# Seven block products for one more group of a fused attention and MLP kernel, with its transposes given to DMA

## The chip, the cores and the metric

The kernel runs on one core of a Trainium2 chip. The metric is the device time of one execution in microseconds. Times of runs are medians; the profile is of one execution, and its span goes from the first to the last instruction.

## The reference

Two layers follow each other. The first is attention with decay, over blocks of 64 positions, for 4 batches, 8 heads, 768 positions and 64 channels. The second normalises the rows of 512 channels and runs a two-layer MLP of width 2048, with a residual:

```
for each block b:
    intra = (q_b k_b^T * Dmask) v_b              # Dmask[i,j] = lam^(i-j) for i >= j, else 0
    inter = (q_b * lam^(pos+1)) @ kv_state
    out_b = intra + inter
    kv_state = lam^64 * kv_state + (k_b * lam^(63-pos))^T v_b
x  = out, heads side by side                     # (4, 768, 512)
xn = (x - mean(x)) / sqrt(var(x) + 1e-6) * g_ln
y  = x + relu(xn @ W1) @ W2                      # W1 512 x 2048, W2 2048 x 512
```

## The kernel before

**Tiling.** The 3072 rows are cut into 12 windows of 256 positions, numbered u = 0 to 11. Window u belongs to batch u mod 4. Each window is a group of two tiles of 128 rows. For each window, attention makes `x` of both tiles, `xc` (centred, times g_ln, bf16) and `xT` (its transpose). Then m1 makes hT = relu(W1^T xT), and m2 multiplies it with W2 and adds x. Windows below 6 (`LB`) use a 128-position form of attention (`kv`, `scores`, `av`, `inter`). Later ones use a 64-position form (`kv64`, `scores64`, `av64`).

**Order.** The order on every engine is written out by hand at the end of the kernel. `plan` is a list of m1 and m2 pieces, called units, of all groups from the second on. `units(n)` issues the next n of them, and the attention steps of later windows stand between such calls. A group has eight m1 units and then eight m2 units. A unit of m1 is 8 matmuls of 256 columns (L530) and one ScalarE relu into hT (L533). The queues of all engines are in order. SP issues nearly all DMAs: loads of k, q and v (`load_in`, L76 and L80), transposes of k and q (`transpose_dma`, L257), transposes of xc (`to_xT`, L486) and stores (L698).

**Attention steps.** The steps `s1` to `s4` treat one window: `s1` has kv and the first scores, `s2` the second scores, `s3` the product with v and the first half of inter, `s4` the second half and the norms. `X1` and `X2` are the same for a later window, with the rest of the window before it. `new_state` and `states64` make the running state: VectorE reads the kv product (`Stmp` L317, or `Smid` L388 and `Stmp` L391), and GpSimd multiplies it with the decay into `Sn` (L313). `reader` copies a few columns of `po` into `seen` (L443), which fences the two halves of inter. `norm` copies po to x on ScalarE (L458) and makes xc on VectorE (L460). `in_k_one`, `in_q_one` and `in_v` cast and scale the loaded inputs into `kq` and `vb` (L231, L236, L242).

**Two forms of m2.** Groups below `WG` use the plain form: for each of the two tiles, 16 matmuls of 512 columns (L666) in four units, and one VectorE eviction of 512 columns (L690). Groups from `WG` on cut h and W2 into 2 x 2 blocks and form seven block products in place of eight:

```python
        products = (("P1", "a", True), ("P2", "b", True), ("P7", "c", True), ("P5", "d", True),
                    ("P6", "a", False), ("P4", "c", False), ("P3", "d", False))
```

A product is 8 matmuls of 256 columns (L565). A unit `m2w(n)` issues 7 of the 56, so a unit's border mostly lies inside a product. The letters are PSUM tiles `pwa` to `pwd`. Each comes from the pool "mm" of four buffers (`mm_tile`), which m1, plain m2, kv and kv64 also use. Three things come in addition. `w_sums(c, n)` forms sums of blocks of W2 once per quarter c (L787 to L791, VectorE, into `wt`). `sums(lo, hi)` (`h_sums`) forms sums of blocks of h for half of the row blocks (L548 to L550, VectorE, into `hs`). `evict` scales each product by rstd and adds it to x (L578 on VectorE; P1 and P7 by ScalarE at L589 and L597, then GpSimd at L590 and L598).

**x^T.** `to_xT` makes it on TensorE for windows below 2 and for those in `X_PE` (four transposes, L493, and a ScalarE copy, L494, for each tile), and else by one DMA transpose for each tile.

Of the kernel before, what the change touches and what calls it, by code (L numbers as in the profile page):

```python
# [17 lines left out]
def kernel(  # L18
# [11 lines left out]
    nc = tc.nc  # L30
# [11 lines left out]
    NWC = 4  # L42
    eps = 1e-6
    XS = 64.0
    WG = 4
    assert D == 64 and S % W == 0 and DM == 512

    ctx.enter_context(tc.manual_schedule())
# [7 lines left out]

    half = [slice(0, 64), slice(64, 128)]
    XB = 3
    X_PE = (2, 3, 4)
    LB = 6  # L60

    def mm_tile(shape, dtype, name):
        return ps.tile(shape, dtype, tag="mm", bufs=4, name=name)
# [8 lines left out]
    def fill(got, name, u, hs, eng=None):  # L72
        eng = eng or nc.sync
        src = dict(k=k, q=q, v=v)[name]
        if u < LB:
            eng.dma_start(got[:, hs], source(src, u, hs))  # L76
            return
        cc, b = divmod(u, B)
        for j in range(2):
            eng.dma_start(got[:, hs, j * D:(j + 1) * D],  # L80
                          src[b, hs, cc * W + j * C:cc * W + (j + 1) * C, :].rearrange("h p d -> p h d"))
# [11 lines left out]
    def load_in(u, name, eng):  # L93
        got = qkv_in[u][name]
        fill(got, name, u, slice(0, H), eng)
        qkv_in[u][name] = got.rearrange("p h (j d) -> p h j d", j=2)
# [54 lines left out]
    def make_keep64():  # L151
        for dst, base in ((keep64, 0), (keep64_b, D)):
            nc.gpsimd.memset(dst, 1.0)
            nc.gpsimd.affine_select(
                out=dst, in_=dst, compare_op=ALU.is_ge, fill=0.0,
                base=base, pattern=[[1, D]], channel_multiplier=-1,
            )
        nc.vector.tensor_copy(keep64[half[1]], keep64_b[half[1]])
# [39 lines left out]
    def open_window(u):  # L198
        kq = wk.tile([128, 2, NP, 2, 2, D], BF16, tag="kq", bufs=3, name="kq")
        vb = wk.tile([128, H, 2, D], BF16, tag="vb", bufs=4, name="vb")  # L200
        st[u] = dict(kq=kq, vb=vb)
        if u < XB:
            st[u]["kqT"] = wk.tile([128, 2, NP, 2, 128], BF16, tag="kqT", bufs=3, name="kqT")

    def part(a, dst, hs):

        return dst[:, a, hs.start // 2:hs.stop // 2].rearrange("p a j e d -> p a e j d")
# [21 lines left out]
    def in_k_one(u, eng, j):  # L229
        src = qkv_in[u]["k"].rearrange("p (a e) j d -> p a e j d", e=2)  # L230
        (eng.copy if eng is nc.scalar else eng.tensor_copy)(part(0, st[u]["kq"], ALL)[:, :, :, j], src[:, :, :, j])  # L231

    def in_q_one(u, eng, j):
        src = qkv_in[u]["q"].rearrange("p (a e) j d -> p a e j d", e=2)
        lq = (lam_q[:, :, j] if u < LB else lam_p[:, 0, :]).rearrange("p (a e) -> p a e", e=2)
        eng.tensor_tensor(part(1, st[u]["kq"], ALL)[:, :, :, j], src[:, :, :, j],  # L236
                          lq[:, :, :, None].to_broadcast([128, NP, 2, D]), op=ALU.mult)
# [200 lines left out]
    def reader(u):  # L438
        s = st[u]
        for ab in range(2):  # L440
            if s["S"][ab][1] is not None:
                seen = wk.tile([128, H], F32, tag="seen", name="seen")
                (nc.scalar.copy if u > WG else nc.vector.tensor_copy)(seen, s["po"][ab][:, :, 0])  # L443

    def norm(u, ab, early=False):
        s = st[u]
# [30 lines left out]
    def to_xT(u, ab):  # L477
        s = st[u]
        t = 2 * u + ab
        g = group_of[t]  # L480
        i = t - groups[g][0]
        if i == 0:
            xT_of[g] = gp.tile([128, KA, GT * 128], BF16, tag="xT", bufs=3, name="xT")
        dst = xT_of[g][:, :, i * 128:(i + 1) * 128]
        if u >= 2 and u not in X_PE:
            nc.sync.dma_start_transpose(dst, s["xc"][:, ab])  # L486
        else:
            if u < 2:
                xt = mm_tile([128, KA, 128], BF16, "xt")
            else:  # L490
                xt = ps.tile([128, KA, 128], BF16, tag=f"po{ab}", name="xt")
            for kk in range(KA):
                nc.tensor.transpose(xt[:, kk, :], s["xc"][:, ab, kk * 128:(kk + 1) * 128], ident)  # L493
            nc.scalar.copy(dst, xt)  # L494
# [18 lines left out]
    m2s = {}  # L513
# [267 lines left out]
    def w_sums(c, n):  # L781
        v = w2[c].rearrange("p (k e) d -> p k e d", e=2)
        w = DM // 2
        b11, b12, b21, b22 = v[:, :, 0, 0:w], v[:, :, 0, w:], v[:, :, 1, 0:w], v[:, :, 1, w:]
        t1, t2, t3, t4 = (wt[c][:, :, i] for i in range(4))
        if n == 0:
            nc.vector.tensor_tensor(t1, b12, b11, op=ALU.subtract)  # L787
            nc.vector.tensor_tensor(t3, b12, b22, op=ALU.add)
        else:
            nc.vector.tensor_tensor(t2, b11, t3, op=ALU.subtract)  # L790
            nc.vector.tensor_tensor(t4, t2, b21, op=ALU.add)  # L791
# [73 lines left out]
    def s2(u):  # L865
        scores(u, 1)
        mask(u, 1)
# [11 lines left out]
    def s4(u):  # L879
        inter(u, 1)  # L880
        if st[u]["S"][0][1] is not None:
            norm(u, 0)
        norm(u, 1)
# [31 lines left out]
    def X2(u):  # L915
        scores64(u)
        inter(u - 1, 1)
        mask64(u, 0)
        norm(u - 1, 0)
        norm(u - 1, 1)  # L920
        mask64(u, 1)
# [20 lines left out]
    in_k(1, nc.gpsimd)  # L942
    norm(0, 0, early=True)
    reader(0)
    behind(qkv_in[1]["k"][:, 0, 0, 0:1])
    load_w1(1)
# [71 lines left out]
    for g in range(2, len(groups)):  # L1018
        m1, m2 = mlp(g)
        plan += [(m1, n) for n in range(m1.count)]  # L1020
        if g >= WG:
            plan += [(m2.w, n) for n in range(8)]
# [5 lines left out]
    def units(n):  # L1028
        for _ in range(n):
            f, *a = next(steps)  # L1030
            f(*a)
# [15 lines left out]
    s3(2)  # L1047
    units(2)
    s4(2)
    open_window(3)  # L1050
    in_k_one(3, nc.vector, 0)
    in_k_one(3, nc.vector, 1)
    in_q_one(3, nc.gpsimd, 0)
    in_q_one(3, nc.gpsimd, 1)
    in_v(3, nc.gpsimd)
# [10 lines left out]
    units(1)  # L1066
    load_in(5, "v", nc.sync)
    units(1)
    open_window(4)
    in_k_one(4, nc.gpsimd, 0)  # L1070
    in_k_one(4, nc.gpsimd, 1)
# [1 line left out]
    in_q_one(4, nc.gpsimd, 1)  # L1073
    in_v(4, nc.gpsimd)
    units(5)
    w_sums(0, 0)
    w_sums(0, 1)
    units(2)
    w_sums(1, 0)
    units(1)  # L1080
    s1(3)
    store(0)
    transpose_dma(4, 0)
    transpose_dma(4, 1)
    units(2)
    s2(3)
    units(1)
    open_window(5)
    in_k_one(5, nc.gpsimd, 0)
# [8 lines left out]
    open_in(6, False)  # L1098
    load_in(6, "k", nc.sync)
    units(1)  # L1100
    load_in(6, "q", nc.sync)
    units(1)
    w_sums(1, 1)
    load_in(6, "v", nc.sync)
    units(1)
    w_sums(2, 0)
    transpose_dma(5, 0)
    units(1)
    make_keep64()
    to_xT(3, 0)  # L1110
    transpose_dma(5, 1)
    open_in(7, False)
    load_in(7, "k", nc.sync)
    units(1)
    w_sums(2, 1)
    s1(4)
    to_xT(3, 1)
    open_window(6)
# [7 lines left out]
    units(2)  # L1126
    s3(4)
    units(1)
    in_q_one(6, nc.vector, 1)
    in_v(6, nc.gpsimd)  # L1130
    s4(4)
    in_q_one(6, nc.vector, 0)
    units(3)
    load_in(7, "q", nc.sync)
    units(1)
    w_sums(3, 0)
    w_sums(3, 1)
    units(1)
    open_in(8, False)
    to_xT(4, 0)  # L1140
    units(1)
    to_xT(4, 1)
    s1(5)
    units(1)
    transpose_dma(6, 1)
# [14 lines left out]
    units(1)  # L1160
    in_k_one(7, nc.scalar, 0)
    units(1)
    X2(6)
    open_window(8)
    units(3)
    m2s[4].sums(0, 4)
    units(1)
    store(1)
# [188 lines left out]
```

## Time and profile before

| what | us |
|---|---|
| median of 4 runs (lowest to highest) | 210.67 (210.46 to 212.09) |
| the profiled execution | 210.66 |
| its span | 208.9 |
| TensorE busy in the span | 198.7 |
| VectorE busy | 138.4 |
| ScalarE busy | 119.0 |
| GpSimd busy | 85.8 |
| mean granted TensorE clock | 0.998 of full speed |

In the profile, PE is TensorE, PEld its weight loads, DVE VectorE, ACT ScalarE, POOL GpSimd and SPq the DMA queue of SP. A row of the timeline has its start and its length in us, the engine, the line, what is written and read with shapes, how many instructions it merges, and in brackets how long the engine was idle before and what ended that. A row of the chain has start, length, what. The chain is followed back from the last instruction, at each step to what released it.

### The profile page before, as it was taken

The page shows a single profiled execution, that of the slowest core. Times are in us where ns is not written, and L with a number is a line of the kernel's source. Part 1 is how long each engine was busy: PE and PEld are TensorE (multiplying, and loading weights), DVE is VectorE, ACT ScalarE, POOL GpSimd, SP SyncE. Part 2 cuts the span into 40 slices and gives each one's busy share as a digit, 9 for nine tenths or more (in the row PEclk, how much of TensorE's full clock was granted, in tenths as well). Part 3 has the DMA queues.
Part 4 walks back from the last instruction along what each step waited for, and adds up shares of the span by engine and source line. Part 5 has one row for each costly group of instructions (what it writes and reads, how often), then busy time and mean ns, then how long its engine had stood idle before and what let it go on. Part 6 is the DMA issues. An engine that isn't in the chain of part 4 may idle for free.

```text
span 208.9 us, 7231 instructions
## 1 busy us (share of the span) xinstructions
PE 198.7 (95%) x3099; PEld 156.6 (75%) x3099; DVE 138.4 (66%) x277; ACT 119.0 (57%) x275; POOL 85.8 (41%) x118
## 2 busy tenths in 40 slices
PE   2889999999999999999999999999999999999992
PEld 0469789545685587478888888888888888888881
DVE  2587580537585776758897776777877947865263
ACT  3834869326254667347566675585596565652620
POOL 4679138219747330626355441782282202011020
PEclk9999999999999999999999999999999999999999
DMA  4999999999999999996899999797958020178403
GB/s 111 297 270 215 201 284 164 192 304 276 186 322 164 219 151 194 192 294 66 175 226 149 196 201 153 195 216 111 236 113 178 3 50 3 25 145 278 111 18 83
DMA packets 91041, 36.38 MB, mean 174 GB/s; under 512 B 65153, under 2 KB 88193, under 8 KB 91010
## 3 DMA queue, kind: packets, MB, share of 16 engines
q1 hardware_dynamic: 86400, 31.53, 74.3%
q0 software_dynamic: 4224, 4.19, 12.7%
q8 instruction: 24, 0.39, 0.8%
q10 hardware_dynamic: 386, 0.20, 0.4%
q14 instruction: 7, 0.06, 0.1%
HBM read 27.27 MB, written 6.29 MB: 161 GB/s over the span
## 4 chain that ended last, share of the span: by engine, by line
PE 78%; DVE 7%; issue 6%; DMA 3%; ACT 2%; POOL 1%; SPq 1%; POOLq 0%; DVEq 0%
PE pm L530 31%; PE pm L666 14%; PE pwa L565 5%; PE pwd L565 5%; PE pwc L565 5%; PE pwb L565 3%; PE pm1t L640 2%; PE po L419 2%; DMA lam_b<-in_lam_dram 2%; PE tp L250 2%; PE po L432 2%; DMA out_dram<-x 1%; PE xt L493 1%; PE sc L273 1%; DVE x L578 1%
## 5 line engine op out<-in xcount | busy, mean ns | idle before, releaser
L530 PE MATMUL pm<-xT,w 128*128 128x256 bf16 x736 | 84.9, 273 | 0.1
L530 PEld LDWEIGHTS <-w 128*128 128x128 bf16 x736 | 70.3, 98 | 9.9 <-issue 0.3
L533 ACT ACTIVATE hT<-pm 128x512 f16<-128x512 f32 x92 | 53.9, 599 | 29.2 <-PE pm L530 29.0
L666 PE MATMUL pm<-w,hT 128*128 128x512 f16 x128 | 30.2, 380 | 0.0
L565 PEld LDWEIGHTS <-hs 128*128 128x128 f16 x256 | 24.9, 98 | 2.9
L313 POOL TENSOR_TENSOR Sn<-Stmp,lam_s 128x256 bf16<-128x256 f32 x16 | 9.8, 616 | 38.6 <-DVE Stmp L317 19.8
L590 POOL TENSOR_TENSOR x<-ev_u,x 128x256 f32<-128x256 f32 x8 | 6.4, 796 | 46.2 <-ACT ev_u L589 46.2
L548 DVE TENSOR_TENSOR hs<-hT 128x1024 f16<-128x1024 f16 x16 | 14.2, 888 | 16.3 <-ACT hT L533 16.3
L565 PEld LDWEIGHTS <-hT 128*128 128x128 f16 x192 | 18.1, 98 | 3.6 <-ACT hT L533 1.6
L666 PEld LDWEIGHTS <-hT 128*128 128x128 f16 x128 | 11.7, 98 | 12.1
L283 DVE TENSOR_TENSOR mA<-sc,keep 128x512 bf16<-128x512 f32 x20 | 13.1, 684 | 6.9 <-PE sc L273 6.9
L458 ACT ACTIVATE x<-po 128x512 f32<-128x512 f32 x18 | 10.6, 590 | 9.7 <-PE po L419 5.3
L460 DVE SCALAR_TENSOR_TENSOR xc<-po,nmean,g_row 128x512 bf16<-128x512 f32 x18 | 12.9, 745 | 3.7 <-ACT nmean L459 3.7
L503 ACT ACTIVATE sq<-x,nmean 128x512 bf16<-128x512 f32 x18 | 12.9, 719 | 0.3
L578 DVE SCALAR_TENSOR_TENSOR x<-pwd,rstd,x 128x256 f32<-128x256 f32 x16 | 7.7, 483 | 8.0 <-POOL x L598 8.0
L242 POOL TENSOR_TENSOR vb<-vin,lam_p 128x1024 bf16<-128x1024 f32 x6 | 11.4, 1898 | 3.2 <-ACT hT L533 3.0
L236 POOL TENSOR_TENSOR kq<-qin,lam_q 128x512 bf16<-128x512 f32 x10 | 10.3, 1046 | 5.7 <-DMA qin<-in_q_dram 5.7
L242 POOL TENSOR_TENSOR vb<-vin,lam_v 128x1024 bf16<-128x1024 f32 (+1 forms) x7 | 11.7, 1675 | 1.4 <-DMA vin<-in_v_dram 1.4
L494 ACT COPY xT<-xt 128x512 bf16<-128x512 bf16 x10 | 5.8, 583 | 9.0 <-PE xt L493 9.0
L550 DVE TENSOR_TENSOR hs<-hs,hT 128x512 f16<-128x512 f16 x16 | 10.1, 628 | 0.5
L578 DVE SCALAR_TENSOR_TENSOR x<-pwa,rstd,x 128x512 f32<-128x512 f32 (+1 forms) x16 | 9.1, 612 | 0.8
L236 POOL TENSOR_TENSOR kq<-qin,lam_p 128x512 bf16<-128x512 f32 x9 | 9.3, 1044 | 1.0 <-DMA qin<-in_q_dram 1.0
(128 smaller groups left out, 300.9 us busy)
## 6 DMA issues: line engine op xcount, KB each, us to landing
out_dram<-x SPq DMA_DIRECT2D x22, 256.0 KB, 3.9
w<-in_moe_w_ch_dram POOLq DMA_DIRECT2D x8, 512.0 KB, 9.2
kin<-in_k_dram SPq DMA_DIRECT2D x14, 256.0 KB, 5.2
qin<-in_q_dram SPq DMA_DIRECT2D x14, 256.0 KB, 5.0
vin<-in_v_dram SPq DMA_DIRECT2D x14, 256.0 KB, 5.2
kin<-in_k_dram SPq DMA_DIRECT2D x5, 512.0 KB, 6.5
qin<-in_q_dram SPq DMA_DIRECT2D x5, 512.0 KB, 8.5
vin<-in_v_dram SPq DMA_DIRECT2D x5, 512.0 KB, 7.8
```

The source lines that it names most:

```text
L236: eng.tensor_tensor(part(1, st[u]["kq"], ALL)[:, :, :, j], src[:, :, :, j], lq[:, :, :, None].to_broadcast([128, NP, 2, D]), op=ALU.mult)
L242: eng.tensor_tensor(st[u]["vb"][:, hs], qkv_in[u]["v"][:, hs], lv.to_broadcast([128, n, 2, D]), op=ALU.mult)
L283: nc.vector.tensor_tensor(s[f"mA{hf}"][:, e], s[f"sc{hf}"][e], kp[:, None, :, :].to_broadcast([128, 2, 2, 128]), op=ALU.mult)
L458: nc.scalar.activation(x, po, ACT.Copy, accum_out=sm)
L460: nc.vector.scalar_tensor_tensor(xc, in0=po, scalar=nm, in1=g_row, op0=ALU.add, op1=ALU.mult)
L503: nc.scalar.activation(sq, s["x"][:, ab], ACT.Square, bias=s["nmean"][:, ab:ab + 1], accum_out=ss[:, ab:ab + 1])
L530: nc.tensor.matmul(pm[:, b, :], lhsT=w1[n // W2K][:, kk, (n % W2K) * 128:(n % W2K + 1) * 128], rhs=xT_of[g][:, kk, 0:N], start=(b == 0 and ...
L533: nc.scalar.activation(hT[:, u * NB:(u + 1) * NB, 0:N], pm, ACT.Relu)
L548: nc.vector.tensor_tensor(s13, b[:, :, 1:2, :].to_broadcast([128, n, 2, 128]), b[:, :, 0:4:3, :], op=ALU.subtract)
L565: nc.tensor.matmul(pr[bank], lhsT=lhs(r), rhs=rhs, start=(first and r == 0), stop=(r == KB // 2 - 1), skip_group_check=True)
L578: nc.vector.scalar_tensor_tensor(out, in0=in0, scalar=r[ab], in1=in1, op0=ALU.mult, op1=ALU.add)
L666: nc.tensor.matmul(acc[i], lhsT=hT[:, kk, i * 128:(i + 1) * 128], rhs=w2[kk // W2K][:, kk % W2K, :], start=(kk == 0), stop=(kk == KB - 1))
```

## The change

From group 3 on (it was 4) m2 has the form of seven products, so windows 3 to 11 use it. The steps of W2's sums stand earlier in the written order and are all issued before the attention of window 4. x^T of window 4 is made by two DMA transposes. With these come other moves. The k casts of window 3 go from VectorE to ScalarE, the q products of window 6 from VectorE to GpSimd, and the fence reads of windows 3 and 4 from VectorE to ScalarE. The DMA transposes of window 4 stand ahead of the load of q of window 7 on SP. `X2(6)` and `open_window(8)` come two units later.

```diff
-    WG = 4
+    WG = 3
...
-    X_PE = (2, 3, 4)
+    X_PE = (2, 3)
...
-                (nc.scalar.copy if u > WG else nc.vector.tensor_copy)(seen, s["po"][ab][:, :, 0])
+                (nc.scalar.copy if u > 2 else nc.vector.tensor_copy)(seen, s["po"][ab][:, :, 0])
...
     s4(2)
+    w_sums(0, 0)
     open_window(3)
-    in_k_one(3, nc.vector, 0)
-    in_k_one(3, nc.vector, 1)
+    in_k_one(3, nc.scalar, 0)
+    in_k_one(3, nc.scalar, 1)
...
     load_in(5, "v", nc.sync)
     units(1)
+    w_sums(0, 1)
     open_window(4)
...
     units(5)
-    w_sums(0, 0)
-    w_sums(0, 1)
-    units(2)
     w_sums(1, 0)
-    units(1)
+    w_sums(1, 1)
+    units(3)
     s1(3)
...
     s2(3)
+    w_sums(2, 0)
     units(1)
...
     load_in(6, "k", nc.sync)
     units(1)
+    w_sums(2, 1)
     load_in(6, "q", nc.sync)
     units(1)
-    w_sums(1, 1)
     load_in(6, "v", nc.sync)
     units(1)
-    w_sums(2, 0)
+    w_sums(3, 0)
     transpose_dma(5, 0)
     units(1)
+    w_sums(3, 1)
     make_keep64()
...
     load_in(7, "k", nc.sync)
     units(1)
-    w_sums(2, 1)
     s1(4)
...
-    in_q_one(6, nc.vector, 1)
+    in_q_one(6, nc.gpsimd, 1)
     in_v(6, nc.gpsimd)
     s4(4)
-    in_q_one(6, nc.vector, 0)
-    units(3)
+    in_q_one(6, nc.gpsimd, 0)
+    units(1)
+    m2s[3].sums(0, 4)
+    units(1)
+    to_xT(4, 0)
+    to_xT(4, 1)
+    units(1)
     load_in(7, "q", nc.sync)
     units(1)
-    w_sums(3, 0)
-    w_sums(3, 1)
+    m2s[3].sums(4, 8)
     units(1)
     open_in(8, False)
-    to_xT(4, 0)
-    units(1)
-    to_xT(4, 1)
+    units(1)
     s1(5)
...
     in_k_one(7, nc.scalar, 0)
     units(1)
+    open_window(8)
+    units(2)
     X2(6)
-    open_window(8)
-    units(3)
+    units(1)
     m2s[4].sums(0, 4)
```

## The prediction

> **What bounds the kernel now.** I read the page's busy line first, then the chain that ended last, then the chain in order of time for the stage that the change rewrites, and at last the timelines of VectorE, GpSimd and the SP queue in that stage.
>
> ```profile
> PE 198.7 (95%) x3099; PEld 156.6 (75%) x3099; DVE 138.4 (66%) x277; ACT 119.0 (57%) x275; POOL 85.8 (41%) x118
> PE 78%; DVE 7%; issue 6%; DMA 3%; ACT 2%; POOL 1%; SPq 1%; POOLq 0%; DVEq 0%
> ```
>
> TensorE is busy 95% of the span and carries 78% of the chain; the rest of the chain lies in the first 15 us and the last 30. A busy TensorE need not be a bound one, so I look whether the chain leaves it in the stage of the change. Columns: start, length, what.
>
> ```profile
> 81.00 0.86 PE pm L666 x4
> 82.09 0.86 PE pm L666 x4
> 83.17 0.38 PE pk L307 x32
> 83.78 2.70 PE pm L666 x12
> 86.82 2.70 PE pm L666 x12
> 89.52 0.64 PE po L419 x64
> 90.59 1.85 PE pm L530 x16
> ...
> 98.52 0.97 PE pwa L565 x8
> 99.49 0.87 PE pwb L565 x8
> ```
>
> It does not: from 81.0 (m1 of the fourth pair, u=3, is done) to 90.59 (m1 of u=4 starts) each piece begins where the last one ends. The 0.23 and 0.22 us holes at 81.86 and 82.95 are the four transposes of x^T each. So here a removed matmul is worth its time, as long as nobody makes TensorE wait. The last two rows show the form that the change brings to this stage: a block product of eight matmuls takes 0.87 us, the first after another kind 0.97.
>
> **The change part by part.** *TensorE, removed and added.* Out go 32 matmuls of 512 columns, 0.86 + 0.86 + 2.70 + 2.70 = 7.12 us, and eight transposes, 0.45 us: 7.57. In come 56 matmuls of 256 columns: 0.97 + 6 x 0.87 = 6.19. Two of the products are cut by attention work of u=5; 2.70 for twelve matmuls is 0.1 over three times 0.867, so each return costs about 0.1: 6.39. Gross saving 7.57 - 6.39 = **1.18 us**. The 24 added weight loads (98 ns in the table of groups) lie under matmuls 109 ns apart.
>
> *Buffers.* The pool "mm" has four PSUM buffers. Plain m2 held one. Products hold two (pwa, pwb) when kv(5) comes, after 14 of 56 matmuls, and takes the other two for pk0 and pk1. The third product, P7 (pwc), must wait until VectorE has read pk0 (Stmp, L317), and P5 (pwd) until it has read pk1. That is a new wait in the middle of TensorE's stream. What stands ahead of it on VectorE are the sums of h.
>
> ```profile
> 83.61 0.42 DVE L317 TENSOR_TENSOR Stmp<-pk,Sn 128x256 f32<-128x256 f32 x1 [1.22 <-PE pk L307]
> ...
> 99.19 0.69 DVE L548 TENSOR_TENSOR hs<-hT 128x1024 f16<-128x1024 f16 x1 [0.97 <-ACT hT L533]
> 99.92 0.43 DVE L549 TENSOR_TENSOR hs<-hs,hT 128x512 f16<-128x512 f16 x1
> 100.38 0.83 DVE L550 TENSOR_TENSOR hs<-hs,hT 128x512 f16<-128x512 f16 x1
> ```
> ```profile
> 84.11 0.61 POOL L313 TENSOR_TENSOR Sn<-Stmp,lam_s 128x256 bf16<-128x256 f32 x1 [6.33 <-DVE Stmp L317]
> ...
> 100.09 0.84 POOL L590 TENSOR_TENSOR x<-ev_u,x 128x256 f32<-128x256 f32 x1 [2.61 <-ACT ev_u L589]
> ```
>
> One triple of sums is 99.19 to 101.21 in u=4's stage: 2.02 us, of which 0.41 is L550 standing behind GpSimd's L590 (0.83 against 0.42 at 97.79). In u=3's stage VectorE ends xc at 80.2, does the first triple to 81.7, and the second from 81.75 (ScalarE's last hT ends at 81.64) to 83.77, since L590 again comes 1.57 us after the first product starts. Then Stmp, 0.42, to 84.15. TensorE wants P7 at 81.00 + 0.97 + 0.65 (six of P2) + 0.61 (kv and scores, 83.17 to 83.78) + 0.32 (two of P2, with the return) = 83.55 and gets it at 84.2: **0.65 stall** (0.25 if L590 misses the triple). P5 needs pk1 read, that needs Sn by GpSimd (0.61), so 84.2 + 0.61, then Stmp, 0.42: 85.35 with two hand-overs, where P7 ends at 85.07: **0.28 stall**. The rest follows: P5 to 86.22, three of P6 and the scores to 86.89, P6 to 87.54, P4 and P3 to 89.28. The next attention step started at 89.52. Net: 1.18 - 0.65 - 0.28 = **0.24 us gained**.
>
> *VectorE behind that wait.* Two L690 (1.5 us) go; the evictions L578 come (four of 0.48, 0.66 and 0.48 = 3.06), behind the masks and in order: the last ends near 90.2. Smid for u=6 then begins 0.24 after m1, as before. I take no further loss; bounds 0 and 0.4 (its slack is one eviction).
>
> *Sums of W2, sooner.* The same 16 operations of 0.42, none added. Two take the place of the k casts at 48.0; two lie in the 2.29 idle before 54.71; four instead of six stand at 55.4; two lie in the 1.34 idle before 63.7; the rest at 66.6 to 70 as now. One that stands behind GpSimd's v product can take 1.42 (the row at 55.37); TensorE wants what is queued behind it (L690 of m2's last tile, done 55.46) at 57.3. Nothing.
>
> *k of u=3 to ScalarE, the fence reads of u=3 and 4 to ScalarE, q of u=6 to GpSimd.* Two casts of 0.61 end at 48.5 on ScalarE, where the x^T copy began at 48.44 and is wanted at 54.5; the reads (0.2) put ScalarE's x copy 0.35 later, its xc is wanted 3.4 us later. GpSimd takes 2 x 1.05 in gaps of 2.97 before and 6.33 after its v product; kq of u=6 is complete at 78.8 instead of 80.8. Nothing; without the gaps it would be 2.1 on GpSimd before Sn.
>
> *x^T of u=4 by DMA.* Two ScalarE copies (0.59) go too.
>
> ```profile
> 76.19 1.41 SPq L80 DMA_DIRECT2D kin<-in_k_dram  x2
> 77.64 2.79 SPq L80 DMA_DIRECT2D qin<-in_q_dram  x2
> 80.86 3.35 SPq L257 DMA_TRANSPOSE kqT<-kq  x2
> ```
>
> SP works in order, and the two transposes stand ahead of q of u=7. They wait for xc (79.4 and 80.2), take 1.2 each on the queue (the rows of L486 at 95.08 and 100.31), and land 2.5 to 5.3 after issue: by 86.1, wanted at 90.35. Behind them q of u=7 is issued 82.0 to 84.8 instead of 77.64 to 80.43, kqT of u=6 84.8 to 88.1, then v, k and four stores (7.6 us) until 95.7; the next x^T is asked for near 96.4. The Trainium skill speaks against this edit: "VectorE: DVE Perf Modes", The three transpose paths, gives 390 ns on TensorE and 1309 ns by DMA for 128x128, and its Rules for kernel authors send such a transpose to TensorE. An estimate by the page: eight cost 3.1 us there against 10.5 by DMA. By the rows TensorE loses 0.45 in all and the DMA pair 2.4 of SP with 4 us to spare, so on a TensorE-bound path the DMA is right, but worth 0.45 and not 3.1. I take the rows. The delay of what is behind costs nothing in my sum: kqT lands 5.7 after issue (as those at 80.86), 92.5 at worst, and its scores are now at 94.0, because they are moved behind four m1 units instead of two. Without that move they would be at 90.35 + 1.85 = 92.2 and 0.3 short.
>
> *X2 of u=6 two units later.* No instruction is added. Norms and masks of u=5 and 6, and VectorE's first sums of u=4 behind them, end 1.75 later against TensorE. Of that the idle 0.97 before 99.19 takes most, and 0.3 comes back because GpSimd is then done (L549 took 0.71 at 97.04 against 0.43 free): the second sums are 0.5 later. TensorE wants their L548 in the middle of P7, 98.52 + 0.97 + 0.87 + 0.44 = 100.8, and it ended at 99.88: 0.4 early still. Bounds 0 and 0.4; I take 0, by that row.
>
> The profiled execution: 210.66 (span 208.9 and 1.76 around it), which is the median of the runs, 210.67. 210.66 - 0.24 = **210.4**. With L590 missing the triple it is 210.0; with 0.4 of each bound lost, 211.2. The likeliest case's own range is 209.9 to 210.9.
>
> **The rivals.** *The whole saving shows* (14%): if VectorE ran Stmp ahead of the sums' end, or the buffers came free otherwise, 210.66 - 1.18 = 209.5. For it: VectorE idled 1.22 us before this very Stmp. Against it: the sums stand there now. *VectorE falls behind for good* (12%): 0.4 at the evictions and 0.4 in u=4's sums, 211.2. For it: 6.3 us added (sums 3.2, evictions 3.06) against 5.8 removed in that stretch. Against it: the idle 0.97. *SP hands over too late, slower* (22%): q of u=7 is issued last at 83.4 and lands 5.2 to 5.6 later, 89.0; GpSimd, in order, makes q of u=7 (2.1, to 91.1) ahead of Sn of u=6, which is wanted at 90.35 + 1.34 = 91.7. A landing over 6.2 us after issue stops Sn, the second Smid, and through the buffers TensorE. The slowest transposes of the trace land after 7.3 and k, q, v of the larger form after 8.5; with 3 us more than 5.6, the price is 3.0 - 0.6 = 2.4 and the time 210.42 + 2.4 = 212.8. For it: DMA near full in every slice from 54 to 90 us. Against it: loads of this form never took over 6.3 in the windows that I read. That the change doesn't do what it says is excluded: the changed program holds 24 matmuls of m2 more, 8 transposes fewer, and two more DMA transposes.
>
> **How the numbers follow.** Likeliest 52%, whole saving 14%, VectorE behind 12%, SP late 22%. Range 209.3 to 212.9: it takes in the whole saving and most of the late case. About 1% (2.1 us) is what a measurement of this kernel can tell from no change: faster by more needs 0.9 us beyond the gross saving, 4% out of that case; slower needs the SP case at its price, 22%; the rest 74%.
>
> **What would show it.** Right: L565 x504, L666 x96; pwc of u=3 starts near 84.2, its wait put down to Stmp; pwd 0.3 after pwc's end; m1 of u=4 near 90.35; no wait of TensorE at the scores of u=6 (94.0). Wrong: P7 without a gap (whole saving), L548 of u=4 after pwc wants it (VectorE), Sn or kqT of u=6 and 7 released by a DMA and TensorE idle at 91 to 104 (SP). Were TensorE to idle before 80, the placing of W2's sums would be the mistake.

## The result and the profile after

| | median, us (lowest to highest) | runs |
|---|---|---|
| before | 210.69 (210.01 to 212.09) | 60 |
| changed | 211.52 (210.69 to 214.12) | 39 |

The ratio is 1.0041, with a 95% interval from 1.0029 to 1.0053: the change costs 0.86 us (0.6 to 1.1), where 0.24 of gain was forecast. It lies inside the forecast's range and within the 1% that the forecast took as too small to tell from no change, but on the wrong side of zero. Ratios, here and below, are of the fast runs alone and medians of all runs, so that a ratio need not be the quotient of its two medians.

The profiled execution of the changed kernel took 212.76 us. The first 37 us are the same program in both kernels, and the profiled executions of all kernels here pass their end (TensorE's 1,021st instruction) at anything from 35.8 to 39.0. In what follows stretches are therefore counted from that instruction: it lies at 36.86 before and at 37.82 after, so 0.96 of the time between the two profiled executions (212.76 to 210.66) is start-up. From there to the end of the last matmul it is 167.97 us before and **168.72** after: 0.75 more, close to the loss of the medians; the remaining 0.4 lies behind the last matmul. Each of these is one execution of its kernel.

The page of the changed kernel: busy times, and the engines' shares of the chain.

```profile
PE 197.7 (94%) x3115; PEld 158.3 (75%) x3115; DVE 143.2 (68%) x280; ACT 120.2 (57%) x280; POOL 89.7 (43%) x122
...
PE 74%; issue 7%; DVE 6%; DMA 4%; POOL 2%; SPq 2%; ACT 2%; POOLq 0%; ACTq 0%; DVEq 0%
```

TensorE has 1.0 us less work, near the 1.18 of the sum of the parts, and the chain has less of it: 74% for 78%. "issue" is up from 6% to 7%. Work went away and idle time came.

The chain of the changed kernel in order of time, in the stage of the new products (start, length, what):

```profile
84.53 0.34 DVE Stmp L317
...
84.94 0.62 POOL Sn L313
...
85.59 0.44 DVE Stmp L317
...
86.07 1.05 PE pwd L565 x8
...
91.25 1.85 PE pm L530 x16
```

and TensorE's timeline there:

```profile
84.91 1.03 PE L565 MATMUL pwc<-wt,hs 128*128 128x256 f16 x8 [0.52 <-DVE Stmp L317]
```

This is the wait that the prediction named: P7 stands 0.52 behind the state sum, and P5 (pwd) is released by the second sum, with GpSimd's Sn between them. m1 of u=4 starts at 91.25, which is 53.43 after the common instruction; before it was 90.59, or 53.73. Up to here the change has **gained 0.30**, where 0.24 was forecast. The loss comes later. The next fence is the chain from there:

```profile
94.86 0.38 PE sc L353 x32
95.23 0.03 PE po L432 x3
95.26 0.72 issue
95.98 0.31 PE po L432 x13
96.29 3.60 PE pm L530 x32
99.89 0.97 PE pwa L565 x8
...
103.26 1.03 POOL x L598
...
104.90 1.15 DVE x L578 x2
...
106.09 0.44 PE pk L372 x31
```

Two places are new. **At 95.26 TensorE stands still for 0.72 us** in the middle of inter(5,1), three of its sixteen matmuls done, and nothing that the profile shows releases it. The products of u=4 start 62.07 after the common instruction, for 61.66 before: 0.71 has been lost since m1's start. At 106.09 the kv products of u=7 wait for VectorE's evictions, and that is another 0.34: m1 of u=5 lies at 70.02 for 69.27. From there to the end nothing changes. The sum is -0.30 + 0.71 + 0.34 = 0.75.

### The profile page after: what moved, and what is told of

Its sections match the earlier page's. It is cut to its first block, busy times and chain, and to the rows that moved or that the text cites. A ratio compares the mean times of both kernels' runs of the same rounds, so it can differ in the third digit from the quotient of the medians.

```text
span 211.0 us, 7281 instructions
## 1 busy us (share of the span) xinstructions
PE 197.7 (94%) x3115; PEld 158.3 (75%) x3115; DVE 143.2 (68%) x280; ACT 120.2 (57%) x280; POOL 89.7 (43%) x122
## 4 chain that ended last, share of the span: by engine, by line
PE 74%; issue 7%; DVE 6%; DMA 4%; POOL 2%; SPq 2%; ACT 2%; POOLq 0%; ACTq 0%; DVEq 0%
PE pm L530 33%; PE pm L666 10%; PE pwa L565 6%; PE pwd L565 6%; PE pwc L565 5%; DMA kin<-in_k_dram 4%; PE pwb L565 2%; PE pm1t L640 2%; SPq L76 2%; DVE x L578 2%; PE po L419 2%; PE po L432 1%; PE tp L250 1%; PE sc L273 1%; PE xt L493 1%
## 5 line engine op out<-in xcount | busy, mean ns | idle before, releaser
L565 PEld LDWEIGHTS <-hs 128*128 128x128 f16 x288 | 27.8, 98 | 4.4 <-issue 0.7
L590 POOL TENSOR_TENSOR x<-ev_u,x 128x256 f32<-128x256 f32 x9 | 7.1, 787 | 52.9 <-ACT ev_u L589 52.9
L548 DVE TENSOR_TENSOR hs<-hT 128x1024 f16<-128x1024 f16 x18 | 15.3, 852 | 15.1 <-ACT hT L533 15.1
L565 PEld LDWEIGHTS <-hT 128*128 128x128 f16 x216 | 20.3, 98 | 4.1 <-ACT hT L533 1.8
L666 PE MATMUL pm<-w,hT 128*128 128x512 f16 x96 | 22.6, 380 | 0.0
L666 PEld LDWEIGHTS <-hT 128*128 128x128 f16 x96 | 8.7, 98 | 9.1
L578 DVE SCALAR_TENSOR_TENSOR x<-pwd,rstd,x 128x256 f32<-128x256 f32 x18 | 8.7, 482 | 8.4 <-POOL x L598 8.4
L236 POOL TENSOR_TENSOR kq<-qin,lam_p 128x512 bf16<-128x512 f32 x11 | 11.3, 1043 | 1.1 <-DMA qin<-in_q_dram 1.1
L597 ACT ACTIVATE ev_p<-pwc,rstd 128x256 f32<-128x256 f32 x9 | 4.3, 474 | 12.9 <-PE pwc L565 12.9
L550 DVE TENSOR_TENSOR hs<-hs,hT 128x512 f16<-128x512 f16 x18 | 10.9, 606 | 0.6
L578 DVE SCALAR_TENSOR_TENSOR x<-pwa,rstd,x 128x512 f32<-128x512 f32 (+1 forms) x18 | 10.3, 613 | 0.8
```

The costliest lines, as they stand in the source:

```text
L548: nc.vector.tensor_tensor(s13, b[:, :, 1:2, :].to_broadcast([128, n, 2, 128]), b[:, :, 0:4:3, :], op=ALU.subtract)
L550: nc.vector.tensor_tensor(s4, s2, b[:, :, 2], op=ALU.add)
L565: nc.tensor.matmul(pr[bank], lhsT=lhs(r), rhs=rhs, start=(first and r == 0), stop=(r == KB // 2 - 1), skip_group_check=True)
L578: nc.vector.scalar_tensor_tensor(out, in0=in0, scalar=r[ab], in1=in1, op0=ALU.mult, op1=ALU.add)
L666: nc.tensor.matmul(acc[i], lhsT=hT[:, kk, i * 128:(i + 1) * 128], rhs=w2[kk // W2K][:, kk % W2K, :], start=(kk == 0), stop=(kk == KB - 1))
```

## The experiments

**The theory.** The list of waits in the changed kernel has two entries of TensorE's matmuls without a releaser:

```profile
PE po L432 <- issue: 0.7, 1, 0.7
PE po L419 <- issue: 0.5, 1, 0.5
```

The first is the gap at 95.26, the second one at 25.96. Counted in TensorE's instructions (weight loads and matmuls), they lie behind number 3,009 and number 705. The distance is 2,304 = 9 x 256. The page lists a DMA queue that belongs to no load of the kernel:

```profile
q8 instruction: 24, 0.39, 0.8%
```

Its 24 packets have 16,384 bytes each, for TensorE's 6,244 instructions. The Trainium skill ("Runtime: NRT & Kernel Launch", Instruction fetch mechanics) says that instructions come in blocks of 16 KiB, which are 256 of them, over a DMA queue of their own, and that crossing the edge of a block costs "one DMA tail-bump, mostly hidden". So theory 1: both gaps are edges of blocks (number 256 n - 63), and TensorE was there before its next block was. The program of the change has 32 more TensorE instructions ahead of this place (48 for the products, less 16 for the transposes), and X2 comes 32 later. Before, edge 12 lay 38 instructions into the m1 matmuls behind X2; now it lies inside inter(5,1). The block ahead of the edge has 64 instructions of m1 and 192 of the small attention matmuls, which pass at some 5 ns each in this trace. Theory 2: X2's new place makes VectorE late. Theory 3: some DMA of the kernel's own is late.

All kernels below were run beside the kernel before on the same chip. "From 37 us" is the stretch from the common instruction to the end of the last matmul, in the profiled execution.

| kernel | median (runs), us | before beside it | ratio (95%) | from 37 us |
|---|---|---|---|---|
| before | 210.69 (60) | | | 167.97 |
| changed | 211.52 (39) | 210.69 | 1.0041 (1.0029 to 1.0053) | 168.72 |
| after_pad108 | 212.92 (6) | 211.11 | 1.0103 (1.0047 to 1.0159) | 167.79 |
| before_pad30 | 212.40 (22) | 211.11 | 1.0022 (0.9994 to 1.0049) | 169.14 |
| x2_back | 212.29 (22) | 211.11 | 1.0059 (1.0038 to 1.0080) | 168.32 |
| kv_po | 211.28 (14) | 211.11 | 1.0013 (0.9986 to 1.0040) | 169.03 |
| after_mid108 | 222.38 (6) | 210.73 | 1.0551 (1.0513 to 1.0589) | 179.29 |
| after_mid128 | 224.09 (6) | 210.73 | 1.0632 (1.0596 to 1.0668) | 181.35 |
| kv_po_mid108 | 221.55 (6) | 210.73 | 1.0503 (1.0468 to 1.0538) | 178.65 |
| x2_back_mid108 | 221.95 (6) | 210.73 | 1.0517 (1.0488 to 1.0547) | 179.10 |
| wg4 | 211.07 (14) | 210.82 | 1.0006 (0.9978 to 1.0035) | 167.30 |
| wg4_x3 | 222.32 (6) | 210.82 | 1.0477 (1.0421 to 1.0534) | 177.74 |
| kv_po_x3 | 223.13 (6) | 210.82 | 1.0529 (1.0479 to 1.0579) | 179.98 |
| xt_pe | 212.97 (8) | 210.82 | 1.0085 (1.0054 to 1.0116) | 170.03 |
| before_x4 | 210.76 (14) | 211.04 | 0.9983 (0.9961 to 1.0006) | 167.80 |
| wg4_x2 | 210.74 (22) | 211.04 | 0.9976 (0.9959 to 0.9993) | 167.40 |

### Moving the edge, and nothing else: after_pad108 and before_pad30

```diff
+    zp = const.tile([128, 64], BF16)
+    nc.vector.memset(zp, 0.0)
...
+    t_pad = ps.tile([128, 64], F32, tag="po0", bufs=1, name="pad")
+    for i in range(108):                 # 30 in before_pad30
+        r = half[i % 2]
+        nc.tensor.matmul(t_pad[r], lhsT=zp[r], rhs=zp[r], start=True, stop=True)
     g_all = ps.tile([128, DM], F32, tag="po1", name="g_all")
```

> The changed kernel with 108 pairs of weight load and matmul of zeros (64x64, into a tile that nothing reads) ahead of everything else on TensorE, in the 4.1 us in which it waits for the first data; nothing else differs, so that every later instruction of TensorE lies 216 places further on in its program. Theory 1 (instruction fetch: the 0.72 us without a releaser at 95.26 is TensorE at the edge of a block of 256 instructions whose fetch has not landed): by the order of issue in the trace the edge now falls about 40 instructions later, in the m1 matmuls behind inter(5,1), and no other edge comes sooner than 4.9 us after the one before it up to 150 us; the gap goes, and most of the 0.34 at kv64(7) with it: 0.6 to 1.0 us less than the changed kernel, so 210.5 to 210.9, level with the kernel before. Theory 2 (the place of X2(6) costs by itself, through VectorE) and theory 3 (a late DMA): 216 more instructions in an idle stretch change nothing, 211.5 within 0.2.

> The kernel BEFORE with 30 pairs of weight load and matmul of zeros (some 1.5 us) ahead of everything else on TensorE, in the 4.1 us in which it waits for data; nothing else differs. Theory 1 (instruction fetch): the edges of the 256-instruction blocks move 60 instructions forward against the program, so that one falls in the dense small matmuls at 92.7, only 2.9 us after the edge before it, and one at 107.5, 3.4 us after the one before; the trace shows 5.2 us as the least from edge to edge there, so TensorE should stand still for up to 2.3 and 1.8 us at these places: 1.3 to 4.5 us slower than before. Theories 2 and 3: no change, within 0.2 us.

TensorE's timeline of after_pad108, at the place of the gap and at 26 us (its lines are numbered six higher):

```profile
26.43 0.19 PE L425 MATMUL po<-vb,mA 64*64 64x64 bf16 x1 [1.56 <-issue]
...
94.56 0.45 PE L359 MATMUL sc<-kqT 64*64 64x64 bf16 x32
94.83 0.30 PE L438 MATMUL po<-Sn,kqT 64*64 64x64 bf16 x16
95.07 3.12 PE L536 MATMUL pm<-xT,w 128*128 128x256 bf16 x27
```

The gap at 95 is gone: all sixteen matmuls of inter run through. From 37 us the kernel is 0.93 shorter than the changed one, as theory 1 had it. It is also 0.18 shorter than before: without the gap the change gains, a little less than the 0.24 of the forecast. But another edge came to lie in the small matmuls at 24 to 26 us, where it was not forecast to cost more than before, and there TensorE stood for 1.56. In the median nothing is won: that half of the expectation failed, and the trace does not say why. It is of the fastest of the six runs (211.60), and its start-up, with the 1.56 in it, is no longer than the changed kernel's (37.60 to 37.82). The others spread to 214.76; in two of them, 213.46 and 213.87, the granted clock was 0.963 and 0.959, where the profiled one had 1.0. So I rest nothing on its median, and the case for theory 1 is made in the traces. The 0.34 at 106 stayed, against the expectation: it is not a consequence of the gap.

before_pad30, the same place:

```profile
91.69 0.23 PE L438 MATMUL po<-Sn,kqT 64*64 64x64 bf16 x5
93.03 0.28 PE L438 MATMUL po<-Sn,kqT 64*64 64x64 bf16 x11 [1.11 <-issue]
```

Sixty instructions of zeros in an idle stretch 90 us earlier put a gap of 1.11 into the kernel *before*, in inter(5,1), where theory 1 said. From 37 us it is 1.17 longer. The size was forecast too large (up to 2.3, and 1.8 at 107.5, where none came), because the fetches began 2.2 and 1.2 us after the edge before, and I had taken 2.9. Its start-up was a microsecond shorter in this execution, with no edge in the small matmuls at 25, which fits that the ratio moves by less than the gap (0.5 us, -0.1 to 1.0, where 1.3 to 4.5 was expected).

### The edge and the fetch

The packets of the instruction queue and TensorE's starts, from the traces, at edge 12 (13 in the kernels with 108 or 128 pairs). In the five kernels that are not listed no two starts there are more than 0.18 apart:

| kernel | edge lies in | edge before crossed | block's fetch | edge crossed | after the fetch's end | longest distance of starts there |
|---|---|---|---|---|---|---|
| before | m1 behind X2 | 89.98 | 92.84 to 93.83 | 95.18 | 1.35 | 0.32 |
| changed | inter(5,1) | 90.53 | 93.29 to 94.61 | 95.98 | 1.37 | 0.91 |
| before_pad30 | inter(5,1) | 88.67 | 90.82 to 91.76 | 93.03 | 1.27 | 1.30 |
| x2_back | m1 behind X2 | 89.18 | 90.61 to 91.93 | 93.23 | 1.30 | 0.91 |
| kv_po | inter(5,1) | 89.27 | 91.83 to 92.92 | 94.22 | 1.30 | 0.29 |
| xt_pe | scores, inter | 90.81 | 92.90 to 94.26 | 95.60 | 1.34 | 0.25 |
| after_mid128 | inter(5,1) | 102.75 | 104.64 to 105.61 | 107.29 | 1.67 | 0.12 |
| after_pad108 | m1 behind X2 | 90.47 | 92.42 to 93.82 | 95.74 | 1.92 | 0.12 |
| wg4 | m1 behind X2 | 90.04 | 92.34 to 93.65 | 95.82 | 2.18 | 0.12 |
| wg4_x2 | m1 behind X2 | 90.19 | 92.33 to 93.64 | 95.86 | 2.22 | 0.11 |
| before_x4 | m1 behind X2 | 91.23 | 92.87 to 94.15 | 96.91 | 2.76 | 0.11 |

Matmuls of m1 start 0.11 apart when nothing holds them. The table falls in two: wherever TensorE stood, it went on 1.27 to 1.37 us after the end of the packet, and wherever it did not stand, it came at least 1.67 after it. Over all 373 edges in the traces of these kernels, no block was entered sooner than 1.22 us after the end of its packet. Every edge with over 0.25 between starts was entered 1.22 to 1.54 after it, but for seven, in kernels with pairs, at which TensorE waits for a sum or is among the pairs (3.3 to 6.4 after it). So some 1.3 us after its packet a block can be used. In the rows in which TensorE stood, the fetch began 1.4 to 2.9 us after the edge before and took 0.9 to 1.4, and the next block was ready 4.1 to 5.5 us after that edge; a block that runs in less leaves a gap, and how large it is differs from trace to trace. Even the kernel before lost 0.2 here.

### X2 alone: x2_back, and the pairs at 40 to 52 us

x2_back is the changed kernel with

```diff
-    open_window(8)
-    units(2)
     X2(6)
-    units(1)
+    open_window(8)
+    units(3)
     m2s[4].sums(0, 4)
```

(Of the two calls only X2 moves against the units; `open_window(8)` sets up tiles and issues no instruction.)

> The changed kernel with X2(6) and open_window(8) back at the place that they have before the change (two units of m1 sooner). Theory 1 (instruction fetch): the edge of the block stays at the same count of TensorE instructions and its data come at the same 95.9, but TensorE now gets there at 93.9 or so, with two units of m1 still to do: the gap is about 2 us instead of 0.72, and the kernel 0.4 to 1.6 us slower than the changed one (211.9 to 213.1). Theory 2 (X2's new place makes VectorE's norms and sums late): what was lost comes back, 0.7 to 1.0 us faster than the changed kernel (210.5 to 210.8).

It ran slower than the changed kernel by the ratios (1.0059 to 1.0041, the intervals overlap), and certainly not 0.7 faster, which would be 1.0008: theory 2 does not carry the loss. The gap stayed, now two matmuls into m1:

```profile
92.20 0.39 PE L530 MATMUL pm<-xT,w 128*128 128x256 bf16 x2
93.23 4.96 PE L530 MATMUL pm<-xT,w 128*128 128x256 bf16 x44 [0.63 <-issue]
```

Theory 1 had the gap at about 2 us; it did not grow because this fetch began 1.43 after the edge and not 2.76. In the trace the kernel is 0.40 shorter than the changed one. Of that 0.14 lies between m1 of u=4 and its products, where the gap is, and 0.29 between those products and m1 of u=5: X2's place is the larger part of the wait at 106.

The mid kernels add the pairs between the 512-column products of the first two pairs:

```diff
                 nc.tensor.matmul(acc[i], lhsT=hT[:, kk, i * 128:(i + 1) * 128], rhs=w2[kk // W2K][:, kk % W2K, :],
                                  start=(kk == 0), stop=(kk == KB - 1))
+                for _ in range(2 if kk < KB - 1 else 0):
+                    j = next(pads, None)     # pads = iter(range(108)), or 128
+                    if j is not None:
+                        r = half[j % 2]
+                        nc.tensor.matmul(acc[i][r, 0:1], lhsT=zp[r], rhs=zp[r, 0:1], start=False, stop=False,
+                                         skip_group_check=True)
```

> The changed kernel with 108 pairs of weight load and matmul of zeros (64x64 by 1 column, added as zeros to the sum that is being made), two after each of the first 54 or so products of 512 columns of the first two pairs, 40 to 52 us. Every later TensorE instruction lies 216 places further on; the block edges before 40 us stay where they are. Theory 1 (instruction fetch): the gap of 0.72 at 95.26 goes and no edge after 52 us comes sooner than 4 us after the one before: 0.7 to 1.0 us less than the control with 128 pairs, in which every edge after 52 us stands where the changed kernel has it. What the pairs cost by themselves is not known; the weight loads lie beside products of 0.217 us, so 0 to 1.5 us for all, and the same in the control to within 0.2. Theories 2 and 3 (X2's place, a late DMA): no difference from the control beyond that 0.2.

> The control: the changed kernel with 128 such pairs, which are 256 instructions, one whole block, so that from 52 us on the block edges fall on the same instructions as in the changed kernel. Theory 1: the gap at the scores of u=6 is there as in the changed kernel (0.7 to 0.9 us), and the time is that of the changed kernel plus what 128 pairs cost by themselves (0 to 1.5 us). Theories 2 and 3: the same.

> Both edits at once: k v products of u=5 in the banks of po, and the 108 pairs at 40 to 52 us. If the two stalls at P7 and P5 (0.74) and the gap at the block edge (0.72 and some of the 0.34 behind it) are separate losses, the time is 0.5 to 0.8 below that with the 108 pairs alone and 1.2 to 1.7 below the control with 128: if the pairs cost nothing, 209.8 to 210.2 against 210.7 for the kernel before. If they hide each other, one of the two edits adds under 0.3.

> The 108 pairs at 40 to 52 us with X2(6) and open_window(8) at their place of before: no block edge then lies in or near X2, so that what is left is the cost of X2's place by itself. Theory 1 (the fetch is all of it): within 0.35 of the changed kernel with the same 108 pairs, on either side. Theory 2 (the place of X2 makes VectorE late): 0.4 to 1.0 us faster than it.

The pairs were not nearly free, where 0 to 1.5 was expected: 11.5 us for 108, by the stretch from 37 us against after_pad108. The control did not do its work either. In after_mid128 the edge lies in inter(5,1) again, but everything is 11 us later against the DMAs, the fetch began 1.89 after the edge before, and no gap came. So the two kernels differ by their 20 pairs and by little else (2.06 in the trace), and the pair of runs speaks neither for nor against theory 1. It does show that an edge need not cost anything, and how long this block runs when nothing holds it: 4.54 us from edge to edge. x2_back_mid108 is free of the edge: against after_mid108 the place of X2 is worth 0.19 in the trace and 0.4 in the medians, whose intervals overlap. kv_po_mid108 is 0.64 below after_mid108 in the trace and 0.8 in the medians (the intervals just overlap): the stalls at P7 and P5 cost this also where no gap is, so the two losses are separate.

### The wait for the state sums: kv_po

```diff
     def s1(u):
-        kv(u)
+        kv(u, "po" if u == 5 else "mm")
```

> The changed kernel with the k v products of u=5 in the two banks of po, which nothing uses from 80 to 90 us, instead of two of the four banks that the products of u=3 also take. P7 and P5 then need not wait for the state sums that read those banks: the stalls of 0.52 and 0.22 us at 84.9 and 86.1 should go. Theory 1 (the stalls lie on the path to the end): 0.6 to 0.8 us less than the changed kernel, 210.7 to 210.9, with the gap at the block edge kept, since the fetch starts from the edge before it and moves along. Rival (the time is hidden, because the av of u=5 then waits for its masks or for the state): no change within 0.2 us, with a wait at 89.5 to 91.

```profile
83.68 1.04 PE L565 MATMUL pwc<-wt,hs 128*128 128x256 f16 x8
84.56 1.04 PE L565 MATMUL pwd<-wt,hs 128*128 128x256 f16 x8
...
146.03 0.61 PE L565 MATMUL pwc<-wt,hs 128*128 128x256 f16 x4 [1.23 <-DVE hs L548]
```

P7 and P5 follow without a gap; against the changed kernel 0.71 is gained between 83 and 88 us, and 0.60 of it is left at m1 of u=4. The medians point the same way: 1.0013 for 1.0041, which is 0.6 us, though the intervals overlap. So the two stalls were on the path, at 0.6 to 0.7 together, where the prediction charged 0.93. (The row at 146.03 is peculiar to this execution: a load of q landed late, VectorE waited 3.74 for it, and 1.4 was lost. Without it the stretch from 37 us would be 167.6.)

### The parts alone: wg4, xt_pe, before_x4, wg4_x2

wg4 is the changed kernel with these edits; wg4_x2 has those of x2_back in addition. before_x4 and xt_pe change `X_PE` alone, before_x4 in the kernel before.

```diff
-    WG = 3
+    WG = 4
...
-    m2s[3].sums(0, 4)
...
-    m2s[3].sums(4, 8)
```

> The changed kernel with WG = 4 and without the h sums of u=3, so that u=3 keeps its eight block products of before; x^T of u=4 by DMA, the earlier W2 sums, the k casts and the place of X2(6) stay as the change has them. Against the kernel before it is x^T by DMA and the moves alone. TensorE does 0.73 us more than in the changed kernel (7.12 of products for 6.39), P7 and P5 have nothing to wait for (0.74 less), and its program is 48 instructions shorter there. Theory 1 (instruction fetch): the block edge then lies in the m1 matmuls behind X2, with more of them in the block, and no gap is left at 95: 210.1 to 210.5, 0.2 to 0.6 below the kernel before and about 1.2 below the changed one. Theory 2 (the place of X2 costs by itself): the loss of 0.7 to 1.0 stays, 211.2 to 211.6.

> The changed kernel with x^T of u=4 back on TensorE: the part of the change that is x^T by DMA undone. Its eight transposes cost 0.45 us on TensorE; the program is 16 instructions longer ahead of X2, and the block edge falls at the end of the scores of u=6, with the gap kept at 0.3 to 0.9. Both theories: 0.2 to 0.6 us above the changed kernel, 211.7 to 212.1. If x^T by DMA costs something that was not seen (SP's queue, the DMA engines' time): 0 to 0.5 below the changed kernel.

> The kernel BEFORE with x^T of u=4 by DMA and nothing else. Eight transposes of 0.45 us leave TensorE; its program is 16 instructions shorter ahead of X2, so that the block edge of 95 falls 16 instructions later and 0.7 us further from the edge before it. The prediction's costing (x^T by DMA frees 0.45 and costs nothing): 210.2 against 210.7. With the instruction fetch (the gap of 0.32 at 95.18 goes as well): 0.6 to 0.8 less, 209.9 to 210.1. If DMA's x^T costs something that was not seen: no gain.

> The changed kernel with WG = 4, without the h sums of u=3, and with X2(6) and open_window(8) back at their place of before: x^T by DMA, the W2 sums, the casts and the copies for seen stay moved. If these moves cost nothing, as forecast: the same as x^T by DMA alone within 0.2, from 38 us to the end 0.6 to 0.8 less than the kernel before. If X2's place costs 0.15, as the two kernels with the 108 pairs show: 0.1 to 0.2 less than with WG = 4 alone in the trace. If the moves cost (GpSimd and VectorE in each other's way): up to 0.7 above x^T by DMA alone.

wg4: 0.67 less than before from 37 us, with no gap at the edge, as expected; the runs do not show it (+0.1 us by the ratio, -0.5 to +0.7, where 0.2 to 0.6 below before was expected). wg4_x2 has the same trace to 0.1 and runs below before: **0.9976, 0.9959 to 0.9993, which is 0.5 us faster than the kernel before and 1.4 faster than the changed one.** It is the best kernel of this study. before_x4, with x^T by DMA alone, comes out the same within the intervals (0.9983), which is 0.4 us for the 0.6 to 0.8 that was expected. Its trace is 0.4 longer than that of wg4_x2; all of that is one wait of the scores for a mask at 61.9,

```profile
62.25 0.41 PE L273 MATMUL sc<-kqT 64*64 64x128 bf16 x15 [0.36 <-DVE mA L283]
```

and from 64 us to the end the two traces stay within 0.1 of each other. So the moves of W2's sums, casts and fence reads cost nothing that these traces show. X2's place does: from m1 of u=4 to m1 of u=5, where neither kernel has a gap, wg4 takes 15.37 us and wg4_x2 15.20, and after_mid108 takes 15.42 and x2_back_mid108 15.27. That is 0.17 and 0.15. (Over the whole stretch it does not show between wg4 and wg4_x2, because the latter waited 0.2 longer near 61 us, ahead of everything that X2 touches.)

xt_pe cost more than expected: 0.9 us by the ratios and 1.3 in the trace, for 0.2 to 0.6. In the order of the change the transposes stand before their xc is there, and TensorE waits 0.19 and 0.41 for it; with the transposes themselves the products of u=3 start 1.4 later.

### One x^T more by DMA: wg4_x3 and kv_po_x3

Both set `X_PE = (2,)`, on top of wg4 and of kv_po.

> The same with x^T of u=3 by DMA as well (eight transposes of 0.45 us less on TensorE, two DMA transposes more in SP's queue behind the loads of u=6, due before m1 of u=3 at 73). If TensorE is the bound there and the DMA comes in time: 0.3 to 0.5 us below the kernel with WG = 4 alone, 209.6 to 210.2. If SP's queue is late (x^T of u=3 landing after 73, or k^T, q^T of u=5 pushed back by 2.5 us): 0 to 1.5 us above it.

> The changed kernel with k v of u=5 in the banks of po and x^T of u=3 by DMA. Its TensorE program is 16 instructions shorter ahead of X2, and the block edge falls in inter(5,1) as before, some 14 instructions from its end: the gap there stays, at 0.3 to 0.9. Theory 1: 0.3 to 0.5 below the kernel with k v in po alone, so level with the kernel before or 0.3 below it; if SP's queue is late, as in the run before: 0 to 1.5 above.

Both lose 11 us. SP's queue of kv_po_x3, and TensorE:

```profile
70.41 3.79 SPq L257 DMA_TRANSPOSE kqT<-kq  x1
74.30 1.21 SPq L486 DMA_TRANSPOSE xT<-xc  x1
...
78.27 1.44 SPq L486 DMA_TRANSPOSE xT<-xc  x1
```
```profile
81.83 1.89 PE L530 MATMUL pm<-xT,w 128*128 128x256 bf16 x8 [10.34 <-DMA xT<-xc]
```

x^T of u=3 stands behind a transpose of k, q of u=5 in the written order; that one waits for its casts on GpSimd, and SP with it. m1 wanted x^T at 71.5. I had read the queue's free time and not what it waits for. Not all of the 11 us is the wait itself. The granted clock was 0.5 from 75.2 to 85.5, in wg4_x3 from 76.7 to 87.0, where the other kernels have 1.0 throughout this stage. The first eight matmuls of m1 took 1.81, counted until what follows them starts, where eight took 0.98 at 87.44. Compared in this way, the work up to 86.67 took some 1.7 longer, on top of the 10.34. For u=4 the same edit is in the right place: there the pair was issued at 80.25 and landed in 2.4.

## Why the prediction was wrong

The step that failed is "No instruction is added ... I take 0", with the fetch of TensorE's instructions left out: at the block edge the change lost 0.71. A second 0, for VectorE behind the moved X2, came out as 0.34. The rest of the sum held.

**Right: the products and their wait.** The counts are as said (288 + 216 weight loads at L565, 96 at L666). Forecast 0.65 for P7 and 0.28 for P5; counted in the same way, from start to start and against kv_po, where neither waits, it was 0.68 (2.26 from P2 to P7 for 1.58) and 0.29 (1.17 from P7 to P5 for 0.88). The profile's own idle time at P7 is 0.52, less, because it counts from the modelled end of the matmul ahead. Forecast 0.24 net at m1 of u=4, measured 0.30. kv_po shows both that the wait was real and what it cost: some of it, 0.26, comes back at the next scores, which wait in kv_po. The seven products of u=3 save 0.73 of TensorE time and lose more in it: from m1 of u=3 to m1 of u=4 the changed kernel takes 18.26 us and wg4, which has the eight products of before, 17.97. On their own they cost 0.29 here. The forecast has 0.73 - 0.93 = -0.20 for them.

**Right: x^T by DMA, SP's queue, W2's sums.** SP's queue in the changed kernel, to be held against the three rows of before:

```profile
80.25 2.51 SPq L486 DMA_TRANSPOSE xT<-xc  x2
82.81 1.20 SPq L80 DMA_DIRECT2D qin<-in_q_dram  x2
84.12 4.35 SPq L257 DMA_TRANSPOSE kqT<-kq  x2
```

With the start-up taken off, the load of q of u=7 comes 4.2 us later than before and the transposes of u=6 2.3 later, and no wait for either shows at 91 to 104; the rival of the late hand-over did not happen. The stretch from m1 of u=3 to m1 of u=4 shows the worth: 18.52 us before and 17.97 in wg4 and wg4_x2, 0.55 for the 0.45 that was forecast. So the gain at m1 of u=4 is x^T's, less what the products cost.

**Wrong: "X2 of u=6 two units later. No instruction is added... I take 0, by that row."** Taken by itself the 0 was 0.15 to 0.17 too low, inside its bounds of 0 to 0.4. What was missing is that the step, together with the 32 more instructions of the others, changes *which* instruction is the first of a block. I counted 24 added weight loads and hid them under matmuls, which is right for their execution; their fetch I did not count. The block ahead of the edge went from one that runs in 4.98 us (before: 5.19 with 0.21 of gap) to one that runs in 4.54 (after_mid128), so 0.44 of the added loss is the change's. The rest of the 0.7 is this execution's fetch, ready 5.45 us after the edge before for 5.19. The sign "no wait of TensorE at the scores of u=6" failed with it. That the gap is the edge's is shown, in the traces, by after_pad108 (gone, with nothing else changed) and before_pad30 (made, with nothing else changed). That after_pad108 comes so near to the forecast is in part luck: the 0.34 below, which the sum put at 0, is set off by the 0.2 that the kernel before lost at its own edge, which the sum did not know of.

**Half wrong: VectorE behind X2.** The rival "VectorE falls behind for good" was priced at 0.8, and 0.34 of it came, at another place than it named. VectorE and GpSimd of the changed kernel, and GpSimd's row of before:

```profile
101.59 0.91 DVE L549 TENSOR_TENSOR hs<-hs,hT 128x512 f16<-128x512 f16 x1
...
103.28 0.42 DVE L231 CAST kq<-kin 128x512 bf16<-128x512 f32 x1
...
103.26 1.02 POOL L598 TENSOR_TENSOR x<-ev_p,x 128x256 f32<-128x256 f32 x1 [1.03 <-ACT ev_p L597]
```
```profile
101.83 0.73 POOL L598 TENSOR_TENSOR x<-ev_p,x 128x256 f32<-128x256 f32 x1 [0.91 <-ACT ev_p L597]
```

The sums were in time for P7, but L549 took 0.91 beside GpSimd's L590, the cast fell on GpSimd's L598 (1.02 for 0.73), and the evictions behind them held the buffers of kv64(7). From the products of u=4 to m1 of u=5 the changed kernel takes 0.35 more than before, x2_back 0.06 more; wg4 0.17 more, wg4_x2 0.01. So most of it is X2's place, inside the bounds of 0 to 0.4. That the cast beside L598 is what slows it is read from these rows and was not tested.

**Open.** How much of the loss of the medians is the gap is not shown: the kernel that is without it by padding alone has no better median, and wg4 and wg4_x2, which have it in neither trace, differ from the changed kernel in the products too. How large the gap is in the runs without a profile is not known (there is one trace of each kernel); the larger spread of the changed kernel (214.12 at most, for 212.09) would fit a gap that varies, but was not shown to be that.

## What to carry to other kernels

A gap on TensorE that no semaphore explains should be counted in instructions: if two of them lie a multiple of 256 apart, the fetch is the first suspect, and the packets of the instruction queue beside it tell. Wherever TensorE stood at an edge here, the next block could be used 4.1 to 6.0 us after the edge before; a stretch that runs 256 instructions sooner is where it bites. An edit that adds or removes TensorE instructions moves every later edge, so a change of half a microsecond has to be judged with the edge moved as well, or it is judged by luck. And before a product is given to a new form, look at who still holds the buffers that it rotates into: here that wait took back the whole saving, and two idle banks of another pool removed it (kv_po).

## What the hardware showed that was not expected

Instruction fetch was not always hidden. The rule quoted above ("mostly hidden") holds in the changed kernel for all but two edges, and fails at those in blocks of mostly 64 x 64 matmuls, where TensorE stood for up to 1.56 us.

A tiny matmul between large ones is dear. TensorE's timeline of after_mid108:

```profile
46.19 0.19 PE L675 MATMUL pm<-zp 64*64 64x1 bf16 x2
46.31 0.39 PE L669 MATMUL pm<-w,hT 128*128 128x512 f16 x1
```

A pair of 64 x 64 by one column between products of 512 columns cost 106 ns (11.5 us for 108), while 108 pairs by 64 columns among themselves took 3.09 us at the start, 29 ns each. So it is not the columns that cost. Whether it is the change of form or the shared accumulation (the pairs add to the sum that the large ones are making), no run separates.
